# Second copies of q's and k's high parts: casts replaced by SBUF-to-SBUF transfers

## The chip, the cores and the metric

The kernel runs on one core of a Trainium2 chip. The metric is the device time of one execution in microseconds (us), as the median of several runs. TensorE (PE in the profile, PEld for its weight loads), VectorE (DVE), ScalarE (ACT), GpSimd (POOL) and SyncE (SP) run side by side; transfers are issued here from SP's queue.

## The reference

Block-causal attention over 8 batches of 8 heads, 576 positions and 64 columns a head, and then a gated MLP without a nonlinearity:

```python
scores = scale * np.matmul(q, k.transpose(0, 1, 3, 2))      # scale = 1/8
mask = block_i >= block_j                                   # blocks of 64 positions
scores = np.where(mask, scores, -1000000000.0)
attn = np.exp(scores - max); attn = attn / (sum + 1e-09)
attn_out = np.matmul(attn, v)
x = attn_out as [4608, 512]
out = ((x @ w1) * (x @ w2) @ w3) @ w_out                    # 512 -> 1024 -> 1024 -> 512
```

All inputs are float32.

## The kernel before

**Split numbers.** TensorE reads numbers of a shortened float32 (`F32R`). To keep accuracy, a number is cut into a high part, which is its rounding, and a low part, the rest. A cast to `F32R` makes the high part; a GpSimd subtraction makes the low part. A product is then the sum of several.

**The score product.** Heads go in pairs; head `j` of a pair has its 64 rows of q and k on its own half of the 128 partitions (`own[j]`; the other half is `oth[j]`). Two tiles per head of a pair let one product over 128 partitions do two of these products at once. `hi[j]` holds q high and k high on the own half, q high and k low on the other. `lo[j]` holds q low and k high on the own half, and on the other half rows that shift and mask the scores: a constant part and a row of negated maxima, `lo<-ms`, which a small transfer on SP brings for each head (line 199, `shift`). A score tile is the sum of `hi` and `lo` products (line 235). So q's high part stands twice in `hi[j]`, on both halves, and k's high part stands on the own half in `hi[j]` and in `lo[j]`.

**Who fills these tiles.** `prep_qk(n, j)` has three steps for pair `n` and head `j`. The first casts q and k together on the own half (64x1152). The second casts q's high part on the other half (64x576) and subtracts for k low. The third casts k's high part into `lo[j]` (64x576) and subtracts for q low. The tuple `CAST` says whether ScalarE or VectorE makes each rounding: the first and second step are VectorE's, the third is ScalarE's. For pairs 1 to 4 all casts go to ScalarE. All of these casts stand on line 160 in the profile, since the helper `cast` issues them.

**Stages.** For the first four pairs (`EARLY`) the weights come in: each piece is loaded as float64 words into one of five buffers `wraw` and turned into float32 by four operations of VectorE (`wbits`, lines 139 to 144). After that the other 28 pairs run with the MLP of the batch before between their products; from 987 us on only the last batch's MLP is left. In a late pair the steps of the two heads are: score products (`S`), exponentials on ScalarE (`p` or `rsum`, line 250, and `ph`, line 251), low parts of these on VectorE (`pl`, line 253), the product with the values (`V`, line 291), the sums (`tr`, `part` on VectorE, lines 304 and 305, and the product `tot`, line 309), and the normalization. `M` makes the maxima of the next pair (`m` on VectorE, line 186), `A` is `prep_qk` of the next pair's first head, `B` that of the own second head, `F` one step of the MLP, where ScalarE copies `a`, VectorE multiplies to `g` (line 395) and ScalarE rounds that to `gh` (line 396).

**Order.** TensorE's order in the late part is the one written in `PLAN`. On the other engines, and on SP's queue, the order is written at build time by the framework's planner, from estimated durations and the order in which the program names the operations; every engine and queue then works strictly in that order. The planner moves `prep_qk` forward: its casts stand where the earlier reader of the tile has just ended.

The raw q, k, v of a pair come in one transfer into one of two buffers (line 94); the constants of the mask use one of these two at the start. Results leave by 64 stores, `out_t<-o`.

Of the kernel before, what the change touches and what calls it, by code (L numbers as in the profile page):

```python
# [7 lines left out]
F32 = mybir.dt.float32  # L8
# [6 lines left out]
PSUM = bass.MemoryType.PSUM  # L15
# [3 lines left out]
BLK = 64  # L19
NB = S // BLK  # L20
NPAIR = H // 2
# [4 lines left out]
NF = DF // P  # L26
HALF = S // 2
RAW = 2 * S + 640
EARLY = NPAIR  # pairs whose work is spread over more engines while the weights come in
SCALE = 0.125  # L30
BIG = 8.0e9

# Columns of a head's probabilities (keys on partitions): a chunk of 128 keys
# takes the queries that may see it; zeros keep every product 256 columns wide.
PC = [128, 704, 1152, 1536, 1920]
PW = 1984
QLO = [0, 128, 256, 384, 512]
# The same without zeros, less the first query.
PE = [0, 448, 768, 960, 1024]


# Order of a head's steps, for the first and the second head of a pair.
PLAN = (
    "B F B F S F S B F F S S F F F S M M V F V V V F R F F V Q N",
    "M A S S A F F S F M M S F F F S M A M V V V F V F F V N Q F R T M F F",
)
# The same for the pairs before the first product of the MLP, while the weights come in.
EARLY_PLAN = (
    "M S S S C S C C C C M S V V B C M M V A V M V M Q B M A B M N",
    "S C C S A S S C S C V V V V V Q N T",  # L50
)
# Steps of the first pair with the MLP beside it that leave the MLP's place empty.
DELAY = 3
# Whether ScalarE makes the roundings of (q and k, q, k, k for the maxima, q for the maxima, v).
CAST = (0, 0, 1, 1, 1, 1)


@with_exitstack
def block_causal_attention__then__gated_mlp_kernel(ctx, tc, qkv, consts, ident_in, w1, w2, w3t, wout, out_t):
    nc = tc.nc  # L60
# [14 lines left out]
    w1l = cpool.tile([P, NC, DF], F32R, name="w1l")  # L75
    wh = cpool.tile([P, NF, DM], F32R, name="wh")
    wl = cpool.tile([P, NF, DM], F32R, name="wl")
    # Per head of a pair: (q, k) with high parts on the head's own half of the
    # partitions and q high, k low on the other; and (q low, k high) on the own
    # half with the rows that shift and mask the scores on the other.  # L80
    hi = [cpool.tile([P, 2, S], F32R, name=f"hi{j}") for j in range(2)]
    lo = [cpool.tile([P, 2, S], F32R, name=f"lo{j}") for j in range(2)]
    w2h = cpool.tile([P, NC, DF], F32R, name="w2h")
    w2l = cpool.tile([P, NC, DF], F32R, name="w2l")
    # Queries of both heads of a pair, block by block on a diagonal.
    qd = cpool.tile([P, NB, P], BF16, name="qd")
    own = [slice(0, D), slice(D, P)]
    oth = [slice(D, P), slice(0, D)]
# [12 lines left out]
    for j in range(2):  # L101
        nc.vector.tensor_copy(lo[j][oth[j]], cst[0:D, 0 : 2 * S].rearrange("p (t s) -> p t s", t=2))
    nc.gpsimd.memset(qd, 0.0)
    # Tiles of the time while the weights come in, and those that take their bytes.
    tl = {}

    def open_early(pool):
# [3 lines left out]
    def open_late():  # L111
        pool = ctx.enter_context(tc.tile_pool(name="late", bufs=1, reuse_waits="tile"))
        tl["late"] = pool
        tl["ph"] = pool.tile([P, PW], F32R, name="ph")
        tl["sum"] = pool.tile([P, S], F32, name="rsum")
        tl["pl"] = pool.tile([P, PW], F32R, name="pl")
        # Values: high part on the columns of the head's own half, low part on the other.
        tl["vs"] = [pool.tile([P, 5, P], F32R, name=f"vs{j}") for j in range(2)]
        for t in (tl["ph"], tl["pl"]):
            for a, b in ((0, PC[0]), (PC[2] + 320, PC[3]), (PC[3] + 192, PC[4])):  # L120
                nc.gpsimd.memset(t[:, a:b].bitcast(F32), 0.0)
        tl["gh"] = pool.tile([P, NF, HALF], F32R, name="gh")
        tl["gl"] = pool.tile([P, NF, HALF], F32R, name="gl")

    def load_w(dst, src, k):
        """512 columns of float64 words (low, high), as float32.

        Magnitudes below float32's smallest normal become zero.
        """
        t = tl["early"].tile([P, 1024], F32, tag="wraw", name="wraw", bufs=5)  # L130
        u = tl["early"].tile([P, 512], F32, tag="wbits", name="wbits", bufs=6)
        wide = t.bitcast(I32)
        nc.sync.dma_start(out=wide.rearrange("p (k w) -> p k w", k=k), in_=src)
        wide = wide.rearrange("p (c two) -> p c two", two=2)
        low, high = wide[:, :, 0], wide[:, :, 1]
        bits = u.bitcast(I32)
        V = nc.vector
        nc.scalar.activation(u, high.bitcast(F32), AF.Abs)
        V.tensor_scalar(out=u, in0=u, scalar1=2.0**-15, scalar2=None, op0=ALU.max)
        V.tensor_scalar(out=bits, in0=bits, scalar1=3, scalar2=0x3FFFFFF8, op0=ALU.logical_shift_left, op1=ALU.bitwise_and)  # L140
        V.scalar_tensor_tensor(out=bits, in0=high, scalar=-0x40000000, in1=bits, op0=ALU.bitwise_and, op1=ALU.bitwise_or)  # L141
        if dst is None:
            dst = u.unsqueeze(1)
        V.scalar_tensor_tensor(out=dst.bitcast(I32), in0=low.rearrange("p (k w) -> p k w", k=k), scalar=29,
                               in1=bits.rearrange("p (k w) -> p k w", k=k), op0=ALU.logical_shift_right, op1=ALU.bitwise_or)
        return u
# [17 lines left out]
    def shift_mask(n):  # L164
        r = raw_of[n]
        rqk = r[:, 0 : 2 * S].rearrange("p (t s) -> p t s", t=2)
        kb = work.tile([P, S], BF16, tag="kb", name=f"kb{n}")
        cast(n, kb, rqk[:, 1, :], CAST[3])
        for j in range(2):
            cast(n, qd[own[j], :, own[j]], rqk[own[j], 0, :].rearrange("p (i r) -> p i r", r=BLK), CAST[4])  # L170
        yield
        m = work.tile([P, 32], F32, tag="m", name=f"m{n}")

        groups = [((7, 0, 512),), ((8, 0, 512),), ((6, 0, 448), (0, 0, 64)), ((5, 0, 384), (1, 0, 128)),
                  ((4, 0, 320), (2, 0, 192)), ((3, 0, 256), (8, 512, 576))]
        for g, parts in enumerate(groups):
            t = ps_q.tile([P, 512], F32, tag="psq", name=f"mx{n}_{g}")
            at = 0
            done = []
            for i, a, b in parts:  # L180
                sc = t[:, at : at + b - a]
                nc.tensor.matmul(sc, qd[:, i, :], kb[:, a:b], start=True, stop=True)  # L182
                done.append((sc, 9 if a else i))
                at += b - a
            for sc, col in done:
                nc.vector.reduce_max(m[:, col : col + 1], sc, axis=AX.X)  # L186
            yield
        nc.vector.tensor_tensor(out=m[:, 8:9], in0=m[:, 8:9], in1=m[:, 9:10], op=ALU.max)
        mt = ps_q.tile([P, 512], F32, tag="psq", name=f"mt{n}")
        nc.tensor.transpose(out=mt[0:NB, 0:P], in_=m[:, 0:NB], identity=ident)  # L190
        ms = work.tile([16, P], F32R, tag="ms", name=f"ms{n}")
        nc.scalar.mul(out=ms[0:NB], in_=mt[0:NB, 0:P], mul=-1.0)
        ms_of[n] = ms
        shift(n, 0)
        yield
# [5 lines left out]
    def prep_qk(n, j):  # L201
        rqk = raw_of[n][:, 0 : 2 * S].rearrange("p (t s) -> p t s", t=2)
        o, x = own[j], oth[j]
        if j == 1:
            shift(n, 1)
        cast(n, hi[j][o], rqk[o], CAST[0])
        yield
        cast(n, hi[j][x, 0, :], rqk[o, 0, :], CAST[1])
        nc.gpsimd.tensor_tensor(out=hi[j][x, 1, :], in0=rqk[o, 1, :], in1=hi[j][o, 1, :], op=ALU.subtract)  # L209
        yield  # L210
        cast(n, lo[j][o, 1, :], rqk[o, 1, :], CAST[2])
        nc.gpsimd.tensor_tensor(out=lo[j][o, 0, :], in0=rqk[o, 0, :], in1=hi[j][o, 0, :], op=ALU.subtract)
        yield

    def prep_v(n, j):
        rv = raw_of[n][:, 2 * S :].rearrange("p (j c d) -> p j c d", j=2, c=5)[:, j]
        if n < EARLY:
            if n == 0:
                tl["ve", j] = tl["early"].tile([P, 5, P], F32, name=f"ve{j}")
                nc.gpsimd.memset(tl["ve", j][:, :, oth[j]], 1.0)  # L220
            nc.scalar.copy(tl["ve", j][:, :, own[j]], rv)
            return
        v = tl["vs"][j]
        cast(n, v[:, :, own[j]], rv, CAST[5])
        nc.gpsimd.tensor_tensor(out=v[:, :, oth[j]], in0=rv, in1=v[:, :, own[j]], op=ALU.subtract)

    def s_tile(n, j, parts, p_early):
# [34 lines left out]
        [(2, 256, 576, 256)],  # L262
        [(3, 320, 576, 384), (4, 512, 576, 512)],
    ]
    # (chunk, first column of the probabilities, width, first column in PSUM)
    PV = [(0, 0, 256, 256), (0, PC[0] + 128, 448, 512), (1, PC[1], 448, 512), (2, PC[2], 320, 640),
          (3, PC[3] - 64, 256, 704), (4, PC[4] - 192, 256, 704)]

# [30 lines left out]
    x_of = {}  # L299

    def sums(n, j, part):
        """Sums over the keys: 32 by 32 transposes, then over the groups of 32 partitions."""
        tr = work.tile([P, S], F32, tag="tr", name=f"tr{n}_{j}")
        nc.vector.transpose(tr, tl["sum"])  # L304
        nc.vector.reduce_sum(part[:, j, :], tr.rearrange("p (b c) -> p b c", c=32), axis=AX.X)  # L305
# [120 lines left out]
    weights = gen_w(wp)  # L426

    def pair(n):
        """The attention of a pair of heads, with what the plan places between its steps."""
        early = n < EARLY  # L430
        x32 = work.tile([P, S], F32, tag="x32", name=f"x32_{n}")
        rr = work.tile([P, S // 32], F32, tag="rr", name=f"rr{n}")
# [52 lines left out]
    open_late()  # L485
    for j in range(2):
        prep_v(NPAIR, j)
    # Products of the gated MLP stand between those of the attention, which wait for other engines.
    ctx.enter_context(tc.manual_schedule(engines={mybir.EngineType.PE}))
    mlp = (None for b in range(B - 1) for _ in gen_moe(b))  # L490
    for n in range(NPAIR, NN):
# [52 lines left out]
```

## Time and profile before

| | |
|---|---|
| runs | 1067.49, 1069.15, 1069.55 us; median 1069.15 |
| span of the profiled execution | 1066.6 us, 18267 instructions |
| TensorE busy | 986.9 us (93%) |
| VectorE busy | 810.3 us (76%) |
| ScalarE busy | 594.9 us (56%) |
| GpSimd busy | 601.4 us (56%) |
| transfers | 61.52 MB; SP's queue uses 17.0% of 16 engines |

The span is the time from the first to the last instruction of one profiled execution; the runs, timed without a profile, also hold what lies around it, and are 0.9 to 2.9 us longer. Rows name a line of the kernel, an engine, an operation and `out<-in` by the program's tile names; idle time of an engine stands with what ended it. Matmuls overlap each other, so that a busy TensorE is not one at its peak.

### The profile page before, as it was taken

The numbers are of one execution on the slowest core, as the hardware profiler recorded it, in microseconds if no ns is written. First come the engines' busy times: TensorE is split into PE (matmuls) and PEld (weight loads), VectorE is DVE, ScalarE is ACT, GpSimd is POOL, SyncE is SP. The second block draws the span as 40 slices with busy tenths as digits, with TensorE's granted clock in tenths as the row PEclk, the third lists the DMA queues.
The fourth block names the chain that finished last, engine by engine and source line by source line (L and its number), as shares of the span: only waits on it lengthen the run. The fifth ranks groups of instructions, "written<-read, shape, count | busy, mean of one in ns | idle before, by whom it ended". The sixth has DMA issues, their size and how long they took to land.

```text
span 1066.6 us, 18267 instructions
## 1 busy us (share of the span) xinstructions
PE 986.9 (93%) x6624; PEld 892.7 (84%) x6624; DVE 810.3 (76%) x1432; ACT 594.9 (56%) x1505; POOL 601.4 (56%) x631
## 2 busy tenths in 40 slices
PE   3789778999999999999999999999999999999998
PEld 1444347999998989999999989899999999899998
DVE  7999997878787887778787888877787878886100
ACT  4646566656665656556565656565565656554221
POOL 3324367656575666666565756666665657564211
PEclk9889889999999999999999999999999999999999
DMA  6665421111111001111111110111111111000000
GB/s 214 202 194 191 140 73 36 35 58 36 58 35 54 18 34 47 41 52 36 58 36 58 36 47 19 39 47 42 52 36 58 35 59 36 22 3 18 7 24 23
DMA packets 27196, 61.52 MB, mean 58 GB/s; under 512 B 3361, under 2 KB 19873, under 8 KB 27105
## 3 DMA queue, kind: packets, MB, share of 16 engines
q1 hardware_dynamic: 27104, 60.35, 17.0%
q8 instruction: 52, 0.85, 0.3%
q14 instruction: 40, 0.32, 0.1%
HBM read 50.76 MB, written 9.44 MB: 56 GB/s over the span
## 4 chain that ended last, share of the span: by engine, by line
PE 47%; DVE 34%; ACT 11%; issue 6%; DMA 1%; POOL 1%; ACTq 0%; DVEq 0%; SPq 0%; POOLq 0%
PE ab L388 21%; PE o L404 12%; DVE pl L253 6%; PE s L235 6%; DVE m L186 4%; DVE hi L160 3%; DVE part L305 3%; DVE tr L304 3%; ACT ph L251 3%; DVE g L395 2%; PE x L291 2%; ACT p L250 2%; PE mx L182 2%; PE w L365 2%; DVE wbits L141 2%
## 5 line engine op out<-in xcount | busy, mean ns | idle before, releaser
L256 POOL TENSOR_TENSOR rsum<-rsum,p 128x448 f32<-128x448 f32 x224 | 176.7, 789 | 124.1 <-ACT p L250 116.6
L253 DVE TENSOR_TENSOR pl<-p,ph 128x448 fp32r<-128x448 f32 x168 | 149.1, 901 | 62.2 <-ACT ph L251 61.3
L397 POOL TENSOR_TENSOR gl<-g,gh 128x288 fp32r<-128x288 f32 x128 | 107.5, 840 | 138.0 <-ACT gh L396 135.6
L396 ACT CAST gh<-g 128x288 fp32r<-128x288 f32 x128 | 55.5, 433 | 228.2 <-DVE g L395 228.2
L235 PE MATMUL s<-hi 128*128 128x288 f32 (+4 forms) x384 | 127.8, 344 | 29.0 <-ACT ph L251 21.4
L388 PE MATMUL ab<-xh,w2h 128*128 128x288 f32 x512 | 153.3, 300 | 0.1
L404 PE MATMUL o<-gh,wh 128*128 128x288 f32 x512 | 152.1, 297 | 0.0
L388 PE MATMUL ab<-xh,w1h 128*128 128x288 f32 x512 | 150.9, 295 | 1.1 <-ACT xh L339 1.1
L388 PE MATMUL ab<-xl,w1h 128*128 128x288 f32 x512 | 151.0, 295 | 0.5 <-POOL xl L340 0.5
L388 PE MATMUL ab<-xh,w2l 128*128 128x288 f32 x512 | 150.9, 295 | 0.0
L388 PE MATMUL ab<-xh,w1l 128*128 128x288 f32 x512 | 150.9, 295 | 0.0
L388 PE MATMUL ab<-xl,w2h 128*128 128x288 f32 x512 | 150.9, 295 | 0.0
L404 PE MATMUL o<-gh,wl 128*128 128x288 f32 x512 | 150.8, 295 | 0.0
L404 PE MATMUL o<-gl,wh 128*128 128x288 f32 x512 | 150.7, 294 | 0.0
L186 DVE TENSOR_REDUCE m<-mx 128x1 f32<-128x512 f32 (+6 forms) x320 | 128.1, 446 | 5.0 <-PE mx L182 3.2
L251 ACT ACTIVATE ph<-s 128x288 fp32r<-128x288 f32 x336 | 131.3, 393 | 0.0
L209 POOL TENSOR_TENSOR hi<-raw,hi 64x576 fp32r<-64x576 f32 x64 | 93.7, 1464 | 43.2 <-ACT hi L160 17.8
L291 PE MATMUL x<-ph,vs 128*128 128x256 f32 x336 | 111.6, 340 | 0.1
L250 ACT ACTIVATE p<-s 128x448 f32<-128x448 f32 x224 | 85.4, 381 | 44.6 <-PE s L235 44.3
L235 PE MATMUL s<-lo 128*128 128x288 f32 (+4 forms) x384 | 107.0, 307 | 2.2 <-DMA lo<-ms 1.2
L235 PEld LDWEIGHTS s<-hi 128*128 128x128 f32 (+1 forms) x384 | 70.9, 185 | 45.5 <-ACT ph L251 28.0
L395 DVE TENSOR_TENSOR g<-ab,a 128x288 f32<-128x288 f32 x128 | 57.4, 448 | 66.4 <-PE ab L388 65.5
(77 smaller groups left out, 2558.7 us busy)
## 6 DMA issues: line engine op xcount, KB each, us to landing
raw<-in_qkv SPq DMA_DIRECT2D x32, 896.0 KB
out_t<-o SPq DMA_DIRECT2D x64, 144.0 KB
wraw<-in_w3t SPq DMA_DIRECT2D x16, 512.0 KB
wraw<-in_w SPq DMA_DIRECT2D x16, 512.0 KB
wraw<-in_wout SPq DMA_DIRECT2D x8, 512.0 KB
lo<-ms SPq DMA_DIRECT2D x64, 2.2 KB
cst<-in_consts SPq DMA_DIRECT2D x1, 288.0 KB
ident<-in_ident SPq DMA_DIRECT2D x1, 128.0 KB
```

What stands on the lines that cost most here:

```text
L186: nc.vector.reduce_max(m[:, col : col + 1], sc, axis=AX.X)
L209: nc.gpsimd.tensor_tensor(out=hi[j][x, 1, :], in0=rqk[o, 1, :], in1=hi[j][o, 1, :], op=ALU.subtract)
L235: nc.tensor.matmul(t[ks, at : at + q1 - q0], src[:, 1, kr], src[:, 0, q0:q1], start=(s == 0), stop=(s == 1))
L250: nc.scalar.activation(p32, t[ks, at : at + w], AF.Exp, scale=SCALE)
L251: nc.scalar.activation(ph[ks, o : o + w], t[ks, at : at + w], AF.Exp, scale=SCALE)
L253: nc.vector.tensor_tensor(out=low, in0=p32, in1=ph[ks, o : o + w], op=ALU.subtract)
L256: nc.gpsimd.tensor_tensor(out=r, in0=r, in1=p32, op=ALU.add)
L291: nc.tensor.matmul(xps[:, to : to + w], v[:, c, :], pr[:, a : a + w], start=(u < 2 and s == 0), stop=(u in (0, len(PV) - 1) and s == len(p ...
L388: nc.tensor.matmul(t[:, 0:HALF], l[:, c, fs], r, start=(c == 0 and s == 0), stop=(c == NC - 1 and s == 2))
L395: nc.vector.tensor_tensor(out=g32, in0=acc[1][:, 0:HALF], in1=a32, op=ALU.mult)
L397: nc.gpsimd.tensor_tensor(out=gl[:, f, :], in0=g32, in1=gh[:, f, :], op=ALU.subtract)
L404: nc.tensor.matmul(t[:, 0:HALF], l[:, f, es], r[:, f, :], start=(f == 0 and s == 0), stop=(f == NF - 1 and s == 2))
```

## The change

`prep_qk` casts once, on the own half, and the two other places of the high parts are filled by transfers from there. Both are issued in the second step: q high to the other half of `hi[j]`, k high to the own half of `lo[j]`. The third step keeps only its subtraction. `CAST` loses two entries, and the rest keep their engines. Everything else in the diff removes comments.

```diff
-# Whether ScalarE makes the roundings of (q and k, q, k, k for the maxima, q for the maxima, v).
-CAST = (0, 0, 1, 1, 1, 1)
+CAST = (0, 1, 1, 1)
...
-        cast(n, kb, rqk[:, 1, :], CAST[3])
+        cast(n, kb, rqk[:, 1, :], CAST[1])
...
         cast(n, hi[j][o], rqk[o], CAST[0])
         yield
-        cast(n, hi[j][x, 0, :], rqk[o, 0, :], CAST[1])
+        nc.sync.dma_start(out=hi[j][x, 0, :].bitcast(F32), in_=hi[j][o, 0, :].bitcast(F32))
+        nc.sync.dma_start(out=lo[j][o, 1, :].bitcast(F32), in_=hi[j][o, 1, :].bitcast(F32))
         nc.gpsimd.tensor_tensor(out=hi[j][x, 1, :], in0=rqk[o, 1, :], in1=hi[j][o, 1, :], op=ALU.subtract)
         yield
-        cast(n, lo[j][o, 1, :], rqk[o, 1, :], CAST[2])
         nc.gpsimd.tensor_tensor(out=lo[j][o, 0, :], in0=rqk[o, 0, :], in1=hi[j][o, 0, :], op=ALU.subtract)
         yield
...
-        cast(n, v[:, :, own[j]], rv, CAST[5])
+        cast(n, v[:, :, own[j]], rv, CAST[3])
```

More of the change, by code (lines that the diff above doesn't have):

```diff
@@ L167, in shift_mask @@
         kb = work.tile([P, S], BF16, tag="kb", name=f"kb{n}")
-        cast(n, kb, rqk[:, 1, :], CAST[3])
+        cast(n, kb, rqk[:, 1, :], CAST[1])
         for j in range(2):
-            cast(n, qd[own[j], :, own[j]], rqk[own[j], 0, :].rearrange("p (i r) -> p i r", r=BLK), CAST[4])
+            cast(n, qd[own[j], :, own[j]], rqk[own[j], 0, :].rearrange("p (i r) -> p i r", r=BLK), CAST[2])
         yield
```

## The prediction

> **What bounds the kernel now.** I read a table by stretch first, then the tensor engine's rows with their idle time, then the chain of waits, because only the chain tells whose work a saved cast shortens.
>
> ```profile
> 0.00:170.00 170.00, 126.53 (x392) 69.00 (x393) 152.29 (x256) 100.85 (x192) 72.65 (x61) 0.89 0.49 159
> 170.00:987.00 817.00, 783.97 (x5658) 747.56 (x5658) 650.67 (x1161) 477.11 (x1273) 514.94 (x554) 1.00 0.12 40
> ```
>
> Columns of the stretches: length, busy time of PE, PEld, DVE, ACT, POOL, granted clock, DMA share, GB/s. There are two kernels in one. Up to 170 us VectorE is the fullest (152 of 170) while the weights come in. From 170 to 987 us TensorE is busy 784 of 817, so 33 us is all that can be won there unless matmuls vanish, and none does. Where those 33 us lie, in that same stretch:
>
> ```profile
> L235 PE MATMUL s<-hi 128*128 128x448 f32 x334 | 103.5, 320 | 21.4 <-ACT ph L251 21.4
> L291 PE MATMUL x<-pl,vs 128*128 128x256 f32 x280 | 91.6, 330 | 3.7 <-DVE pl L253 3.6
> L309 PE MATMUL tot<-part,ident 128*128 128x36 f32 x56 | 9.9, 260 | 7.7 <-DVE part L305 7.7
> ```
>
> And its waits (us in total, times, longest):
>
> ```profile
> PE s L235 <- ACT ph L251: 21.4, 27, 0.8
> PE tot L309 <- DVE part L305: 7.7, 13, 0.6
> ```
>
> 21.4 + 3.7 + 7.7 = 32.8 us: nearly all. The score product of the third tile waits 27 times, once a pair, 0.79 us for an exponential; the product of the sums waits 13 times, every second pair, 0.59 us for VectorE. The chain of waits shows what stands behind the first (second head of a pair; start, length, what):
>
> ```profile
> 647.72 0.71 DVE hi L160
> 648.44 0.75 DVE part L305
> 649.20 0.38 DVE g L395
> 649.60 0.03 ACT gh L396
> ...
> 651.49 0.31 ACT ph L251
> 651.84 0.67 PE s L235 x2
> ```
>
> ```profile
> 649.60 0.43 ACT L396 CAST gh<-g 128x288 fp32r<-128x288 f32 x1 [3.44 <-DVE g L395]
> ```
>
> By its own timeline (second fence) ScalarE is idle 3.44 us for `g`, and `g` stands on VectorE right behind a cast `hi` of 0.71 us: the copy of q's high part for the next pair's first head, which nobody needs before 665 us (below). It is prefetch work standing in an urgent place. The chain of the other stall, and that of the pair after it:
>
> ```profile
> 631.98 0.47 DVE hi L160
> 632.46 0.76 DVE part L305
> 633.27 0.41 PE tot L309 x2
> ```
>
> ```profile
> 661.51 1.10 DVE hi L160
> ...
> 676.96 0.70 DVE hi L160
> ...
> 681.07 0.67 PE s L235 x2
> ```
>
> The same cast is on both: 0.47 us ahead of `tot`, and in the following pair 1.10 + 0.70 us ahead of the score product.
>
> **The change part by part.** Removed:
>
> ```profile
> L160 DVE CAST hi<-raw 64x576 fp32r<-64x576 f32 x56 | 42.0, 750 | 1.5
> L160 ACT CAST hi<-raw 64x576 fp32r<-64x576 f32 x8 | 5.3, 669 | 0.2
> L160 ACT CAST lo<-raw 64x576 fp32r<-64x576 f32 x64 | 42.9, 670 | 0.8
> ```
>
> (1) VectorE loses 56 casts, 42.0 us, two a pair. On the path they are worth: in the pairs with a `tot` stall, 0.71 of the 0.79 us at the scores; in the others 0.79 us, since 1.80 us leave their chain and the stall is no longer than that; at `tot` 0.47 of 0.59 us. Taking 14 and 13 of the 27: 14 x 0.71 + 13 x 0.79 + 13 x 0.47 = 9.9 + 10.3 + 6.1 = 26.3 us. At least nothing (if another operation fills the place), at most the 29.1 us of both stalls.
>
> (2) ScalarE loses 64 + 8 casts, 48.2 us. Those of `lo` stand behind the last exponentials of a head, and ScalarE then sits idle for `g` anyway (the 3.44 us above): nothing on the path. If that cover went, it would be 0.67 us twice a pair, again to the good.
>
> (3) At the start the chain runs over VectorE alone, because the second load of q, k, v waits until the casts of constants have freed their buffer:
>
> ```profile
> 6.56 0.45 DVE hi L160
> ...
> 8.92 1.55 DVE hi L160
> ...
> 14.25 4.56 DMA raw<-in_qkv
> ```
>
> The 0.45 and the 1.55 us (second copies of both heads of the first pair) go: -2.0 us, between 0 and -2.0.
>
> Added: 128 transfers of 64 x 576 floats, 147 KB each, on SP's queue. The nearest rows for issue are those of an output store and of the small shift transfers, two of them here:
>
> ```profile
> 635.05 0.34 SPq L409 DMA_DIRECT2D out_t<-o  x1
> ```
>
> ```profile
> 663.00 1.57 SPq L199 DMA_DIRECT2D lo<-ms  x2
> ```
>
> The casts whose results are copied, and a score product that reads them:
>
> ```profile
> 644.10 0.74 DVE L160 CAST hi<-raw 64x1152 fp32r<-64x1152 f32 x1
> 656.78 0.76 DVE L160 CAST hi<-raw 64x1152 fp32r<-64x1152 f32 x1
> ...
> 665.55 0.29 PE L235 MATMUL s<-lo 128*128 128x288 f32 x1
> ```
>
> (4) In the long stretch: for a pair's first head the source is written at 644.84 and its first score product starts just ahead of 665.55, so a copy has 20 us; for the second head (656.78) the reader is a half pair later, so it has more. The whole load of a pair's q, k and v took 4.56 us in (3); at that time for each copy two are in place by 655. Cost nothing; the cover is the early place of the casts, and it would be gone if they slid by more than 10 us. The skill has a price that no row here shows: the Trainium skill, "DMA: Bandwidth & Descriptors", section "Anatomy of one DMA — SWDGE (gpsimd) path", fits 2.0 us + bytes/436e3 per transfer (for the other descriptor path), an estimate of 2.3 us here, three times the cast's 0.75; with it on the path once for each of 56 heads the sum would be some 87 us worse, about 1135 in all. The 20 us of lead speak against that, and it is a rival below.
>
> SP's queue: 0.34 to 0.79 us an issue, four in a pair of 29.2 us (651.84 to 681.07), 1.4 to 3.2 us more. Behind a copy that waits for its cast stand the shift row `lo<-ms`, the stores and the next load. The shift is the tight one: issued at 663.00, its reader at 665.55. Copies whose casts end at 644.84 and 657.5 are gone by then: nothing, at worst 0.7 us a pair if two copies stand just ahead of it (0 to 20 us).
>
> (5) Early stretch: ten heads, 20 copies, 2.9 MB beside 159 GB/s x 170 us = 27 MB. The DMA share there is 0.49 (first table), so mostly hidden; the chain does once wait for a weight load:
>
> ```profile
> 110.32 4.95 DMA wraw<-in_w
> ```
>
> Bounds: 0, and 2.9 MB at 159 GB/s = 18 us if every byte delayed VectorE's next weight. VectorE's own work fills 152 of the 170 us and the loads run ahead of it in five buffers, so I take +2, near the lower end.
>
> (6) The first score products of a head now wait for transfers as well as for engines. An extra wait appears as its own short event:
>
> ```profile
> L160 ACTq EVENT_SEMAPHORE  x29: 17/17/38, 18.8 to 921.2; - x29
> ```
>
> 128 of them at 17 to 38 ns: 2 to 5 us if none overlaps a matmul, below nothing excluded as it is added; I take +2.
>
> (7) What is late next: with TensorE some 0.9 us a pair earlier, `x<-pl` (3.7 us now) waits longer, since `pl` hangs on the exponentials. I allow +3 of the 26.3, from 0 to 10.
>
> By the Trainium skill, "SBUF — State Buffer", section "Who interferes with whom", of a VectorE cast between SBUF tiles and a GpSimd operation the one that starts second is blocked until the other ends. The trace agrees: the same 64x576 cast took 0.45 us at 6.56 and 1.10 us at 661.51, where GpSimd had begun 0.02 us earlier:
>
> ```profile
> 661.49 0.80 POOL L397 TENSOR_TENSOR gl<-g,gh 128x288 fp32r<-128x288 f32 x1
> ```
>
> By that rule GpSimd's work would be shorter too where it now starts second, some further us to the good, and the sum without them stands.
>
> Sum: -26.3 - 2.0 + 0 + 2 + 2 + 3 = -21.3 us. The profiled execution spans 1066.6 us, 2.5 us under the median of 1069.15, so the difference is put on the median: 1069.15 - 21.3, 1048 us.
>
> **The rivals.**
>
> *Everything hidden comes out.* The whole 33 us of idle time go, 2 us at the start with them: 1069 - 35 = 1034. For it: the full 1.80 us in every second pair, more than its stall. Against: `x<-pl` has no cast in its chain.
>
> *Another operation takes the place.* The order on VectorE and ScalarE is written ahead from estimates, so with the cast gone another operation, a reduction or a prefetch of some 0.7 us, can move in ahead of `g`. Then the stall stays: -2 + 4 = +2, 1067 to 1071. Against: in the chain `part` and `g` both wait only for the engine, so both move up.
>
> *The shift row is held up* (slower). If SP's order puts the copies ahead of `lo<-ms` and their cast comes late, the shift waits. From issue to reader it has 2.55 us, of which its issue takes 0.79; of the rest I take 1.0 us as spare, an estimate, since no row gives its landing. Each further us costs a us a pair on TensorE, 28 times. It decides when the shift is later by 1.0 + 26/28, near 2 us, that is when the cast ends after 665 instead of 657.5. At 2.5 us: 28 x 1.5 = 42 against 21: 1069 + 21 = 1090. For it: SP is in order, and VectorE's order may change. Against: 5 us of lead.
>
> *The weight loads are held up* (slower). The 18 us of (5) in full, with half of (1): 18 + 2 - 13 - 2 = +5, 1074. For it: the load of 4.95 us on the chain. Against: one such wait in 170 us.
>
> *The copies land late* (slower). Both issues (0.68 us) and 4.56 us are 5.2 us against a lead of 20; the lead must fall by 15 us, half a pair, before any of it shows. Each us beyond costs 56 us, so 0.5 us brings 28 - 21 = +7, 1076.
>
> **How the numbers follow.** Main case, 1040 to 1058: 0.58. All idle time gone, below 1040: 0.08. Half of it refilled, 1058 to 1067: 0.10. Place taken, within 0.2% (2 us, about what a measurement of this kernel can tell from no change): 0.09. Slower: 0.05 by the shift, 0.08 by the weight loads, 0.02 by late copies. So faster 0.76, same 0.09, slower 0.15. The range leaves out about 1 in 10 at each end: 1036 to 1072; the main case's own is 1040 to 1058.
>
> **What would show it.** Right: the `s<-hi` row's idle time falls from 21.4 to under 6 and `tot`'s from 7.7 to under 3; the pair's period falls from 29.2 to about 28.4 us; VectorE busy falls by some 42, ScalarE by 48; no score product waits for a copy. Wrong: a row of TensorE idle for DMA `hi` or `lo`; ScalarE's wait for `g` as long as before with another operation in front; the first stretch longer than 170 us by more than 4.

## The result, and the profile after

The changed kernel takes 1038.22 us (median of 4 runs, 1035.58 to 1041.36) against 1068.75 us of the kernel before beside it (median of 4 runs, 1067.49 to 1069.55): ratio to the kernel before 0.9718, 95% interval 0.9704 to 0.9732 (every ratio below is to the kernel before, run beside it). It is 30.5 us faster; 1048 us had been forecast, with a range of 1036 to 1072 and 1040 to 1058 for its main case. The profiled execution took 1035.58 us, 1033.8 of them its span; it is the fastest of the four, so times of its first stretch are not typical to the microsecond.

The page of the changed kernel, its first lines, SP's queue and the two new groups of transfers:

```profile
span 1033.8 us, 18491 instructions
PE 980.8 (95%) x6624; PEld 891.9 (86%) x6624; DVE 769.5 (74%) x1376; ACT 546.7 (53%) x1433; POOL 605.3 (59%) x631
q1 hardware_dynamic: 37344, 79.24, 25.4%
hi<-hi SPq DMA_DIRECT2D x64, 144.0 KB
lo<-hi SPq DMA_DIRECT2D x64, 144.0 KB
```

VectorE has 40.8 us less to do than before (810.3), ScalarE 48.2 us less (594.9); the transfers' share rose from 17.0% to 25.4%. These are sums over the whole span, and say nothing yet of the end. The table by stretch does: the first row is from the kernel before, cut at 954 us so that both are the same length, the second from the changed one (length, busy time and instructions of PE, PEld, DVE, ACT, POOL, then granted clock, DMA share, GB/s).

```profile
170.00:954.00 784.00, 751.35 (x5420) 715.66 (x5420) 628.17 (x1125) 461.29 (x1228) 500.39 (x537) 1.00 0.12 42
```

```profile
170.00:954.00 784.00, 778.11 (x5646) 746.12 (x5646) 610.39 (x1104) 439.21 (x1213) 510.44 (x552) 1.00 0.21 61
```

In the same 784 us TensorE is idle 5.9 instead of 32.7 us, and it starts 226 more matmuls. At 784/5646 = 0.139 us each those are 31 us of work: the whole gain. The idle time accounts for 26.8 us of it; the rest was lost while TensorE counted as busy (below, step (1)). The rows that carried the idle time, in that stretch of the changed kernel:

```profile
L235 PE MATMUL s<-hi 128*128 128x256 f32 x332 | 102.6, 320 | 1.9
L291 PE MATMUL x<-pl,vs 128*128 128x256 f32 x280 | 91.6, 330 | 3.8 <-DVE pl L253 3.7
L309 PE MATMUL tot<-part,ident 128*128 128x36 f32 x56 | 9.9, 260 | 0.2
```

The third tile's score product went from 21.4 to 1.9 us, `tot` from 7.7 to 0.2, and `x<-pl` stayed (3.7 and 3.8, over 280 products in both kernels). On VectorE's timeline the reason is plain; first the kernel before, then the changed one, at the same place of a pair (start, length, instruction):

```profile
646.92 0.77 DVE L304 STREAM_TRANSPOSE tr<-rsum 128x576 f32<-128x576 f32 x1
647.72 0.69 DVE L160 CAST hi<-raw 64x576 fp32r<-64x576 f32 x1
648.44 0.75 DVE L305 TENSOR_REDUCE part<-tr 128x18 f32<-128x576 f32 x1
649.11 0.45 DVE L395 TENSOR_TENSOR g<-ab,a 128x288 f32<-128x288 f32 x1
```

```profile
626.51 0.77 DVE L304 STREAM_TRANSPOSE tr<-rsum 128x576 f32<-128x576 f32 x1
627.32 0.75 DVE L305 TENSOR_REDUCE part<-tr 128x18 f32<-128x576 f32 x1
627.99 0.45 DVE L395 TENSOR_TENSOR g<-ab,a 128x288 f32<-128x288 f32 x1
```

From the start of `tr` to that of `g` it is 2.19 us before and 1.48 after: nothing moved into the place. That holds for the whole long stretch: with the casts of the second copies left out of both lists, VectorE (1072 operations), ScalarE (1180) and GpSimd (540) do the same operations in the same order before and after, from 223 us to the end (times of the kernel before). ScalarE's `gh`, and with it the exponential and the score product, follow:

```profile
628.47 0.43 ACT L396 CAST gh<-g 128x288 fp32r<-128x288 f32 x1 [3.28 <-DVE g L395]
```

```profile
630.34 0.29 PE L388 MATMUL ab<-xl,w2h 128*128 128x288 f32 x1
630.71 0.47 PE L235 MATMUL s<-hi 128*128 128x448 f32 x1
```

```profile
650.73 0.29 PE L388 MATMUL ab<-xl,w2h 128*128 128x288 f32 x1
651.84 0.47 PE L235 MATMUL s<-hi 128*128 128x448 f32 x1 [0.82 <-ACT ph L251]
```

The last two fences are TensorE after and before. From the last product of the MLP to the score product it is 0.37 us after and 1.11 before; most neighbours start 0.13 us apart, so little is left of that stall. ScalarE's 3.28 us in front of `gh` are still there and cost nothing now.

**Where the time lies.** The load of q, k and v on SP comes once a pair at the same place of the order. Two of them, eleven pairs apart, cut the span into a first stretch and a steady pace:

```profile
225.14 0.40 SPq L94 DMA_DIRECT2D raw<-in_qkv  x1
...
547.29 0.40 SPq L94 DMA_DIRECT2D raw<-in_qkv  x1
```

```profile
220.92 0.40 SPq L94 DMA_DIRECT2D raw<-in_qkv  x1
...
530.68 0.41 SPq L94 DMA_DIRECT2D raw<-in_qkv  x1
```

Before (first fence) eleven pairs take 322.15 us, after (second) 309.76: 12.39 less, 1.13 us a pair, and 27 pairs at that pace are 30.4 us. Up to the first of the two loads the changed kernel is 4.2 us ahead, some 2 us of it by the pairs of this pace that are already in it. The same two loads were read in every run below:

| kernel | load at | eleven pairs | span |
|---|---|---|---|
| before | 225.14 | 322.15 | 1066.6 |
| changed | 220.92 | 309.76 | 1033.8 |
| q's copies alone by transfer | 221.86 | 309.56 | 1034.3 |
| k's copies alone by transfer | 226.61 | 322.12 | 1068.5 |
| neither casts nor transfers | 226.04 | 309.74 | 1039.0 |
| transfers from pair 5 on only | 223.68 | 309.57 | 1036.6 |
| q's copy half cast, half transfer | 223.01 | 311.13 | 1039.1 |
| q's copy cast by ScalarE | 229.18 | 355.27 | 1146.6 |
| first pair's q copies by transfer | 228.98 | 322.50 | 1071.4 |
| changed, constants apart | 219.49 | 309.78 | 1032.1 |
| q's cast cut in two | 227.11 | 321.15 | 1066.9 |
| q's copies by transfer, constants apart | 223.99 | 309.73 | 1036.4 |

The third column knows few values, whatever the first stretch does: about 322 with the whole cast of q's copy, or two halves of it, on VectorE, about 310 without it, and 355 with it on ScalarE. Kernels of the same pace differ by up to 0.4 us in it. In the long stretch every kernel of the table but the one with the cast on ScalarE has the order of the kernel before on VectorE, ScalarE and GpSimd, apart from the second copies themselves. So a new order by the planner is no rival for the gain.

### The profile page after: what moved, and what is told of

Its sections match the earlier page's. It is cut to its first block, busy times and chain, and to the rows that moved or that the text cites. A ratio compares the mean times of both kernels' runs of the same rounds, so it can differ in the third digit from the quotient of the medians.

```text
span 1033.8 us, 18491 instructions
## 1 busy us (share of the span) xinstructions
PE 980.8 (95%) x6624; PEld 891.9 (86%) x6624; DVE 769.5 (74%) x1376; ACT 546.7 (53%) x1433; POOL 605.3 (59%) x631
## 3 DMA queue, kind: packets, MB, share of 16 engines
q1 hardware_dynamic: 37344, 79.24, 25.4%
## 4 chain that ended last, share of the span: by engine, by line
PE 47%; DVE 29%; ACT 14%; issue 8%; DMA 1%; POOL 1%; DVEq 0%; SPq 0%; ACTq 0%; POOLq 0%
PE o L404 17%; PE ab L388 17%; DVE pl L253 7%; PE s L235 5%; PE x L291 5%; DVE g L395 3%; ACT ph L251 3%; DVE m L186 3%; PE mx L182 2%; ACT xlow L323 2%; DVE wbits L141 2%; ACT p L250 2%; DVE wbits L139 2%; DVE tr L304 2%; DVE ph L253 1%
## 5 line engine op out<-in xcount | busy, mean ns | idle before, releaser
L212 POOL TENSOR_TENSOR lo<-raw,hi 64x576 fp32r<-64x576 f32 x64 | 95.2, 1487 | 26.8 <-ACT hi L160 21.4
```

## The experiments

The theory: a cast of q's high part, needed by nobody soon, stood on VectorE between `tr` and `part`, delayed `part` and `g`, and with them `tot`, the exponential and the score product; its leaving is the gain, and the transfers themselves cost and bring nothing. The rivals credit ScalarE's relief, the start, or the amount of VectorE's work instead of the place of one cast.

**Each copy by itself.** The kernel before with one of the two casts replaced. Only q's:

```diff
-        cast(n, hi[j][x, 0, :], rqk[o, 0, :], CAST[1])
+        nc.sync.dma_start(out=hi[j][x, 0, :].bitcast(F32), in_=hi[j][o, 0, :].bitcast(F32))
```

> Only the copy of q's high part is a transfer; k's copy into lo stays a cast of ScalarE. Theory A (what counts is the 0.7 us cast of VectorE ahead of part and g in every pair): the late stretch gains nearly all of its 27 us, time 1038 to 1044, s<-hi idle in the late stretch under 4 us. Rival B (half of the gain is ScalarE's, which loses 48 us of casts): 1050 to 1060, s<-hi idle 8 to 14 us.

1036.25 us (1036.00 to 1037.87), ratio 0.9714 (0.9698 to 0.9731). That is the whole gain, and 1.8 us below the theory's range, with ScalarE's casts into `lo` all kept; the idle time of its `s<-hi` row is 2.0 us. Only k's:

```diff
+        nc.sync.dma_start(out=lo[j][o, 1, :].bitcast(F32), in_=hi[j][o, 1, :].bitcast(F32))
...
-        cast(n, lo[j][o, 1, :], rqk[o, 1, :], CAST[2])
```

> Only k's copy into lo is a transfer; q's second copy stays a cast of VectorE (ScalarE for pairs 1 to 4). Theory A: the late stretch does not move, s<-hi idle stays 18 to 22 us and tot's 6 to 8; time 1063 to 1070, with what the early stretch gives. Rival B: 1048 to 1058.

1070.52 us (1069.92 to 1073.26), ratio 1.0033 (1.0022 to 1.0045). Its pace is that of before (322.12), and TensorE's rows in the long stretch keep their stalls:

```profile
L235 PE MATMUL s<-hi 128*128 128x448 f32 x322 | 100.0, 321 | 21.4 <-ACT ph L251 21.4
L309 PE MATMUL tot<-part,ident 128*128 128x36 f32 x52 | 9.3, 262 | 8.2 <-DVE part L305 8.2
```

ScalarE's relief is worth nothing there. It is 0.3% slower, 0.5 us above the theory's range; of the 1.9 us between the two profiled spans 1.5 lie before the first of the two loads.

**Without the transfers.** The changed kernel with its two transfers left out and the places that they fill set to zero once; so q's second copy and k's copy beside q's low part are missing from the computation.

```diff
+    for j in range(2):
+        nc.gpsimd.memset(hi[j][oth[j], 0, :].bitcast(F32), 0.0)
+        nc.gpsimd.memset(lo[j][own[j], 1, :].bitcast(F32), 0.0)
...
-        nc.sync.dma_start(out=hi[j][x, 0, :].bitcast(F32), in_=hi[j][o, 0, :].bitcast(F32))
-        nc.sync.dma_start(out=lo[j][o, 1, :].bitcast(F32), in_=hi[j][o, 1, :].bitcast(F32))
```

> Both casts and both transfers are left out; the two places are zeroed once at the start, so the scores lack two of their four terms. What it tells is the price of the 128 transfers. Theory A (transfers are free beside the other work): 1036 to 1040, the same as the changed kernel within 3 us, and its spread is the same. Rival C (SP's queue and the landing cost something, early above all): 1028 to 1034.

1040.93 us (1040.36 to 1041.28), ratio 0.9753 (0.9738 to 0.9768). The pace is 309.74 with no transfers and 309.76 with four a pair. So transfers, SP's issues and the extra waits together cost nothing that can be told from the 0.02 us a pair by which kernels of this pace differ. The time is 0.9 us above the theory's range and far from rival C's. What it loses against the changed kernel, it loses up to the load at 226.04, 5 us later than with the transfers: less work, and a slower first stretch.

**Only in the long stretch.** Transfers for the pairs from 5 on, casts for the others.

```diff
-        cast(n, hi[j][x, 0, :], rqk[o, 0, :], CAST[1])
+        if n > EARLY:
+            nc.sync.dma_start(out=hi[j][x, 0, :].bitcast(F32), in_=hi[j][o, 0, :].bitcast(F32))
+            nc.sync.dma_start(out=lo[j][o, 1, :].bitcast(F32), in_=hi[j][o, 1, :].bitcast(F32))
+        else:
+            cast(n, hi[j][x, 0, :], rqk[o, 0, :], CAST[1])
...
-        cast(n, lo[j][o, 1, :], rqk[o, 1, :], CAST[2])
+        if n <= EARLY:
+            cast(n, lo[j][o, 1, :], rqk[o, 1, :], CAST[2])
```

> Transfers for pairs 5 on, casts as before for pairs 0 to 4. Theory A: the late stretch gains its 27 us as in the changed kernel, the early stretch is as before (first MLP product at 165 to 167 us): 1040 to 1044. Rival D (the late gain depends on how the planner happened to order the early part): late idle of s<-hi over 8 us, 1050 or more.

1037.69 us (1036.70 to 1038.34), ratio 0.9722 (0.9708 to 0.9737), no different from the changed kernel's, and 2 us under the theory's range. The first stretch contributed nothing that these runs can tell.

**Amount or place.** Half of q's copy is cast again by VectorE, beside the transfers of the rest:

```diff
-        nc.sync.dma_start(out=hi[j][x, 0, :].bitcast(F32), in_=hi[j][o, 0, :].bitcast(F32))
+        cast(n, hi[j][x, 0, 0:HALF], rqk[o, 0, 0:HALF], 0)
+        nc.sync.dma_start(out=hi[j][x, 0, HALF:].bitcast(F32), in_=hi[j][o, 0, HALF:].bitcast(F32))
```

> Half a dose: of q's second copy the first 288 columns are cast by VectorE in the old place (about half of 0.7 us), the other 288 come by transfer; the rest as in the changed kernel. Theory A (a stall is as long as the cast in front of g, less what TensorE has to spare): the gap in front of the third score product lies about half way, near 0.7 us between 0.37 (changed) and 1.1 (before); two pairs take 57.3 to 57.8 us against 56.4 and 58.7; time 1050 to 1056. Rival D (the gain came with a new order of the planner, all or nothing): 1036 to 1041, or 1066 and more.

1041.59 us (1041.27 to 1041.92), ratio 0.9746 (0.9731 to 0.9761). Theory A's 1050 to 1056 is missed: the stall did not come back by half, it hardly came back at all (311.13, 0.12 us a pair more than in the changed kernel). The time lies just above the 1036 to 1041 of rival D, but the order is not new (above). VectorE's timeline shows where the half cast went:

```profile
622.65 0.46 DVE L254 TENSOR_TENSOR pl<-rsum,ph 128x288 fp32r<-128x288 f32 x1 [0.43 <-ACT ph L252]
623.99 0.30 DVE L160 CAST hi<-raw 64x288 fp32r<-64x288 f32 x1 [0.87 <-PE s L236]
624.85 2.32 DVE L254 TENSOR_TENSOR pl<-p,ph 128x448 fp32r<-128x448 f32 x2 [0.56 <-ACT ph L252]
```

It stands alone between two waits of VectorE. Of the 52 half casts from the eighth load on 26 stand there, the other 26 directly ahead of a 64x1152 cast, and none ahead of `part`: so this run did not test half a cast in the old place, but half a cast in two other places, where 0.30 us cost next to nothing. The reverse trial keeps both casts in full and no transfer, and only cuts q's cast in two:

```diff
-        cast(n, hi[j][x, 0, :], rqk[o, 0, :], CAST[1])
+        for cs in (slice(0, HALF), slice(HALF, S)):
+            cast(n, hi[j][x, 0, cs], rqk[o, 0, cs], CAST[1])
```

> The kernel before, with both casts kept and no transfer; VectorE's cast of q's high part is only cut into two instructions of 288 columns, which the queue order may place apart. The casting work on VectorE is unchanged (a little more, for the second instruction's own cost). Theory A (what was lost is the 0.45 us by which the cast in front of the summing chain delays that chain; the amount of VectorE's work does not matter): one half, about 0.30 us alone, still stands in front of the part sum in one pair and so the stall shrinks by some 0.15 to 0.6 us in each pair: 1050 to 1062 us. Rival F (VectorE's total work over a pair sets the period): 1068 to 1075 us, no gain. If both halves fall into VectorE's waiting places, 1037 to 1045 us, as with the half cast before.

1071.39 us (1068.76 to 1073.24, 10 runs), ratio 1.0021 (1.0011 to 1.0031): no gain at all, outside what the theory had given it and inside rival F's range. Its timeline:

```profile
618.32 0.77 DVE L305 STREAM_TRANSPOSE tr<-rsum 128x576 f32<-128x576 f32 x1
619.12 0.54 DVE L160 CAST hi<-raw 64x288 fp32r<-64x288 f32 x1
619.69 0.75 DVE L306 TENSOR_REDUCE part<-tr 128x18 f32<-128x576 f32 x1
```

One half stands in the old place (the other halves stand where the half casts of the run before do), and there it takes 0.54 us, four fifths of the whole cast's 0.69, because GpSimd's subtraction runs beside it from 618.07:

```profile
618.07 1.43 POOL L210 TENSOR_TENSOR hi<-raw,hi 64x576 fp32r<-64x576 f32 x1
```

So the chain is only 0.15 us shorter. At the score product that is gained (0.91 to 0.96 us between starts of neighbours on TensorE, from 1.06 to 1.11); at `tot` nothing is (0.88 or 0.89 in 9 of 11 stalls, as before, and longer in two), and some 0.06 us a pair are lost at other products. The pace gains 0.09 us a pair (321.15), and the first stretch loses 2 us. The expectation's 0.30 us for the half was the error. The two runs together answer the question, though not as expected: 288 columns of the same cast cost 0.12 us a pair in other places of VectorE, and keep most of the stall in front of `part`. A rival by which VectorE's total sets the pace gives the right time for this run but the wrong one for the half cast: there VectorE's work between 170 and 954 us rose from 610.39 to 624.68 us, nearly back to 628.17, and eleven pairs took only 1.4 us longer than in the changed kernel.

**The cast on ScalarE.** No transfers; the second entry of `CAST` sends q's copy to ScalarE, so VectorE is relieved as in the change.

```diff
-CAST = (0, 0, 1, 1, 1, 1)
+CAST = (0, 1, 1, 1, 1, 1)
```

> No transfers at all: q's second copy is cast by ScalarE instead of VectorE in every pair. Theory A (only VectorE's place mattered; ScalarE has the 3.4 us in which it waits for g): late gain as in the changed kernel, s<-hi idle under 4 us, 1037 to 1045. Rival E (ScalarE, in order, sits on the same chain, so that 0.67 us more there brings the wait back): 1050 to 1068.

1148.70 us (1148.15 to 1149.75), ratio 1.0749 (1.0733 to 1.0765): far worse than either expectation. ScalarE, GpSimd and VectorE, each by its timeline:

```profile
607.55 0.67 ACT L160 CAST hi<-raw 64x576 fp32r<-64x576 f32 x1 [1.84 <-PE s L235]
608.12 0.32 ACT L250 ACTIVATE p<-s 128x192 f32<-128x192 f32 x1
```

```profile
608.45 1.43 POOL L209 TENSOR_TENSOR hi<-raw,hi 64x576 fp32r<-64x576 f32 x1 [2.06 <-DVE hi L160]
609.96 0.60 POOL L256 TENSOR_TENSOR rsum<-rsum,p 128x192 f32<-128x192 f32 x1
610.64 1.44 POOL L212 TENSOR_TENSOR lo<-raw,hi 64x576 fp32r<-64x576 f32 x1
612.15 0.31 POOL L256 TENSOR_TENSOR rsum<-rsum,p 64x64 f32<-64x64 f32 x1
```

```profile
612.50 0.78 DVE L304 STREAM_TRANSPOSE tr<-rsum 128x576 f32<-128x576 f32 x1 [1.00 <-POOL rsum L256]
```

The cast now stands in front of the last exponentials; their sums on GpSimd come later, and the order has put both subtractions, 1.43 and 1.44 us, ahead of them. In the kernel before the last two sums ran together (1.04 us at 627.90) and the subtractions stood behind, at 629.01 and 630.51. So `tr` waits for GpSimd, and everything behind it is late. In the long stretch TensorE's largest waits are 23.1, 16.9, 16.9, 13.6 and 12.8 us, 83 in all, where the kernel before is idle for 33:

```profile
PE x L291 <- DVE pl L253: 23.1, 26, 0.9
PE ab L388 <- DVE g L395: 16.9, 12, 1.4
PE s L235 <- ACT ph L251: 16.9, 16, 1.1
PE x L291 <- ACT ph L251: 13.6, 24, 0.8
PE tot L309 <- DVE part L305: 12.8, 12, 1.1
```

It refutes the shorter form of the theory, that any place but VectorE's will do, and it fits the longer one, by which a prefetch must not stand ahead of urgent work. It does not show that alone: this is the one run in which the order of VectorE, ScalarE and GpSimd differs in the long stretch, so the 33 us in eleven pairs are the price of the cast's place and of the new order together. ScalarE as such is no bad place: k's copies stood there behind the last exponentials, and taking them away gained nothing.

**The start.** Only the first pair's two copies of q by transfer, all else as before.

```diff
-        cast(n, hi[j][x, 0, :], rqk[o, 0, :], CAST[1])
+        if n == 0:
+            nc.sync.dma_start(out=hi[j][x, 0, :].bitcast(F32), in_=hi[j][o, 0, :].bitcast(F32))
+        else:
+            cast(n, hi[j][x, 0, :], rqk[o, 0, :], CAST[1])
```

> Only the first pair's second copies of q go by transfer, the rest is the kernel before. By step (3) of the prediction the second load is issued some 3 us earlier and the time falls by 2 to 3 us: 1064.5 to 1066.5. Rival: the early stretch swallows it, since VectorE's work on the weights decides, and the time stays within 2 us of before.

1073.32 us (1072.21 to 1074.85), ratio 1.0044 (1.0029 to 1.0059): 5 us above the kernel before (1068.31), which neither the step nor its rival had given. The second load is issued at 11.22 us instead of 14.25, and yet the load at 225.14 comes at 228.98: the 3 us at the start are lost again and more by then.

**The start, pushed further.** The constants of the changed kernel in a buffer of their own, so that the second load waits for nothing.

```diff
-    cst = raws.tile([P, RAW], F32, tag="raw", name="cst")
+    wstack = ExitStack()
+    wp = wstack.enter_context(tc.tile_pool(name="wp", bufs=1))
+    cst = wp.tile([P, 1600], F32, tag="pe", name="cst")
...
-    wstack = ExitStack()
-    wp = wstack.enter_context(tc.tile_pool(name="wp", bufs=1))
```

> The changed kernel with the constants of the mask in a buffer of their own, so that the second load of q, k, v waits for no cast and goes out some 8 us earlier. If the start's chain counts, 1030 to 1035 and the first MLP product moves up by 3 us or more; if VectorE's weights decide, as in the changed kernel, 1035 to 1041.

1035.04 us (1033.14 to 1037.79), ratio 0.9691 (0.9667 to 0.9715); the interval overlaps that of the changed kernel. The second load is issued at 2.26 us instead of 11.24, and yet the first product of the MLP starts at 160.1 us, after 160.7 in the changed kernel: not the 3 us by which it was to move up if the start's chain counted. The same with q's copies alone by transfer, k's second copies being casts of ScalarE again:

> Only q's second copies are transferred (k's second copy stays a cast on ScalarE), and the constants have a place of their own, so that the second load waits for nothing. If the two gains added up: the hi-only kernel's 1036.25 us less up to 3 us, 1033 to 1036 us. If the start's gain is lost in the first stretch, as in the run with the start alone: 1035 to 1042 us, no different from the changed kernel.

1038.11 us (1036.31 to 1041.86), ratio 0.9716 (0.9695 to 0.9737). The gains do not add up: with the load issued early here too, it is no faster than q's copies alone (1036.25). None of these versions is shown to beat the changed kernel.

## Why the prediction was right

The direction and the mechanism were right: `hi` was read from the chain of waits as prefetch work in an urgent place, and that cast alone carries the gain. The size was less good: the main case's own range, 1040 to 1058, is missed by 1.8 us, and a time below 1040 had been given 0.08. Of the signs named ahead, the idle time of `s<-hi` and `tot` (1.9 and 0.2 us), the pair's period (28.2 us) and the busy times came as forecast; ScalarE's wait for `g` stayed nearly as long (3.28 us), but no other operation stands in front. Step by step:

- **(1), VectorE's casts, -26.3 us: right, a little small.** Two pairs were given 0.71 + 0.79 + 0.47 = 1.97 us. By the starts on TensorE the score products gained 0.74 (1.11 to 0.37) and 0.71 us (1.07 to 0.36), and `tot` 0.58 (0.88 to 0.30): 2.03. The pace says 2 x 1.13 = 2.26. The rest lies at three starts in every second pair: the MLP products `ab<-xh,w2h` behind `s<-lo` and `ab<-xh,w2l` behind that, and `x<-ph` behind `x<-pl`. The first two in the kernel before:

```profile
610.17 0.31 PE L235 MATMUL s<-lo 128*128 128x320 f32 x1
610.38 0.40 PE L388 MATMUL ab<-xh,w2h 128*128 128x288 f32 x1
610.61 0.30 PE L388 MATMUL ab<-xh,w2l 128*128 128x288 f32 x1
```

  These gaps between starts are 0.21 and 0.23 us, and 0.15 and 0.13 at the same products of the changed kernel (from 591.33); at `x<-ph` it is 0.28 and 0.19. Over 18 pairs the three give 0.15 us a pair, the score products 0.72 and `tot` 0.29, together the whole 1.16 us of these pairs. A gap shorter than the matmul that is running does not count as idle, so no idle row lists these. All in all 30.4 instead of 26.3 us. That is over the step's upper bound of 29.1, since listed idle time is no upper bound where matmuls overlap; the 33 us of "all that can be won" were read the same way.
- **(2), ScalarE's casts, nothing: right**, by the run with k's copies alone.
- **(3), the start, -2.0 us: wrong.** The load did come 3 us earlier, but the run with that part alone was slower than before. The step ended its account at the load and did not follow what the first 225 us do with it; why they lose it is open (below).
- **(4), the copies and SP's queue, nothing: right.** In the long stretch no product waits for a copy; with or without the transfers the pace is the same to 0.02 us in eleven pairs. The reason given, the lead, held: in the long stretch q's copies are issued some 19 us ahead of their first reader, for both heads of a pair (the step gave the second head more). The estimate of 2.3 us a copy from the fit of the Trainium skill, "DMA: Bandwidth & Descriptors", section "Anatomy of one DMA — SWDGE (gpsimd) path", for the other descriptor path, does not reach the path. The traces record no landing; the nearest to one is the first pair, where the product that waited for the copy starts 3.4 us after the copy's issue (6.70 to 10.09 us), with the constants' and the weights' loads beside it. The 1135 us set beside that price took the cast's 0.75 us off a second time: 56 x 2.3 = 129 us on top of 1048 would have been 1177. SP now waits for the casts, harmlessly, as the waits of the changed kernel show (total us, times, longest):

```profile
SPq L208 <- DVE hi L160: 393.1, 55, 10.8
PE s L235 <- DMA hi<-hi: 1.1, 1, 1.1
```

  The one product that waited for a copy did so at 10 us, in the first pair.
- **(5), the first stretch, +2 us: not settled as a term.** It is not slower after the change (4.2 us ahead at the load), and the run that keeps the casts there has the same ratio. The rival of held-up weight loads (1074) did not occur.
- **(6), extra waits, +2 us, and (7), `x<-pl` next, +3 us: both too large.** (6) is too small to be seen in the pace; the idle time of (7) went from 3.7 to 3.8 us. GpSimd's subtractions for k low, which were to get shorter where they start second, took 1.46 us on average before and 1.47 after.

So the 9.8 us between 1048 and 1038.2 are the 4.1 by which (1) was small and the 7 us of allowances for (5) to (7) that did not come, less the 2.0 of (3), which the runs do not show; the other 0.7 are rounding and the two medians of before (1069.15 and 1068.75). The errors of (1) and of (5) to (7) push the same way, that of (3) the other: the forecast is right by its mechanism and its outer range, not by its sum. The rival "everything hidden comes out" (1034) came closest in outcome, though not for its reason: the start adds nothing, and 5.9 us stay idle. "Another operation takes the place" is excluded for the change by the unchanged order; in the run with q's cast cut in two one half of it keeps the place. Of a held-up shift row and of late copies nothing was seen in the long stretch.

What stays open: why the first stretch moves by several microseconds, from 219.5 to 229.0 us in the table (without the cast on ScalarE), of which the pace explains some 2. It was slower without the transfers than with them, and slower with a start 3 us earlier. The order on several engines changes there at once, and no run takes one of these changes by itself. The one run with the order of the kernel before in its first stretch, that with transfers from pair 5 on, is 1.5 us ahead at the load, no more than its faster pairs account for. Part of the rest may be chance: each stretch was read from one execution, and four runs of the changed kernel alone lie 5.8 us apart.

## What to carry to other kernels

On engines that work strictly in order, look at what stands between an urgent operation and the input it waits for: work that nobody needs soon is worth moving even where the engine is busy only three quarters of the time, and what it is worth is the delay at that place, not its total. Ask of the new place the same question: the same cast cost 1.13 us a pair in front of the sums, half of it 0.12 us in two less urgent places, nothing to be measured as a transfer issued 19 us ahead of its reader, and 3.0 us a pair on ScalarE in front of the exponentials, with the order that came with it. To see whether a change acts in the steady part or in the ramp, time two repeats of one instruction far apart. And where matmuls overlap, compare the starts of the same products before and after: gaps shorter than a matmul show in no idle row.

## What was not expected of the hardware

- 128 transfers of 144 KB inside the chip's SBUF, four a pair of 28.2 us, took no measurable time from the matmuls: eleven pairs took 309.74 us without and 309.76 with them.
- A VectorE cast of 64 x 288 took 0.30 us where GpSimd was idle, and 0.54 us where a GpSimd subtraction was already running, so halving a cast saved only 0.15 us of 0.69. Who starts first counts: with `gl` on GpSimd starting 0.15 us after the half cast it still took 0.30 us, with `gl` starting 0.02 us ahead of it 0.94 (the run with q's cast cut in two).
- Nearly all idle time of TensorE of one kind could go without the next wait growing: 29.1 us listed for two of its rows went to 2.1, and the third stayed at 3.8.
